# First batch's q and k loaded two rows to a partition, a second triangular selection in place of value differences, one more probability buffer, and a new order of the steps

## The chip, the cores and the metric

The kernel runs on one core of one Trainium2 chip. The time is that of one execution on the device in microseconds; the comparison is between the medians of runs of the two kernels. TensorE is called PE below, VectorE DVE, ScalarE ACT, GpSimd POOL, and SyncE, which only starts transfers here, SP.

## What is computed

Two stages, all in fp32 with 4 batches, 768 positions, 8 heads of 64:

```python
scores = (q @ k.T) / 8                     # per batch and head, 768 x 768
keep   = (column < 4) | (0 <= row - column < 128)      # 4 sinks and a window of 128
a      = softmax(where(keep, scores, -1e9));  x = a @ v  # heads side by side: 768 x 512
logits = x @ w_gate                        # 4 experts, the best 2 of each row are kept
for e in experts:                          # causal attention of x with itself, width 64
    y = softmax(causal((x @ wq[e]) @ (x @ wk[e]).T / 8)) @ (x @ wv[e])
    out += weight_of_e * (y @ wo[e])
```

## The kernel before

The work is cut into units: for each batch four "first" units (a pair of heads each, windowed attention) and two "second" units (a pair of experts each), 768 rows as six blocks of 128. Within a first unit, rows 0 and 1 go through `edge_rows`; blocks 2 and 3, and 4 and 5, go together through `both_rows`, so there are 2 x 16 = 32 such bands. The path of a band is: `quarters` (scores by PE in quarters of the array, L1399), `pick` (a copy under a mask, DVE L1729), subtraction of the row's maximum (DVE L1737), the exponential (ACT L1741), normalizing (POOL L1754 or ACT L1752), turning the probabilities by PE (`turned`, L1458), copying them from PSUM into `pt` (L1255 on ACT, L1257 on DVE), one triangular selection by position on POOL (`tri`, L1515), and the product with v (`av`, L1425), which accumulates in PSUM.

A row of block i sees the whole band from block i-1 and block i. Both blocks' scores of a band stand in one 128 columns wide tile, each column holding either the score against block i or the one against block i-1. So the product needs p times v of the right block. Before, it is made as p @ v[i-1] plus (p below or on the diagonal) @ (v[i] - v[i-1]): `differences` makes the tile `dv` with two subtractions per unit on POOL (L1646), and the selection keeps the triangle.

The finished block of a first unit is split into a high and a low part `x` (ACT L1238, then DVE L1243); the second units start from `x` of all four head pairs of a batch: `values` (L1860), then the projections (L1833), causal attention (L1386), and `store` (L1907).

For batch 0 PE turns q and k so that the 64 head dimensions stand on partitions (`turn_by_pe`, L1458 with `ident,qn` or `ident,kn`). For the other batches DVE does it (L1356), from a load that cuts q and k into 32 x 32 blocks (L1801). Batch 0 is loaded at L1797 in packets of one row of 64 numbers, 256 bytes; the first unit in two parts, blocks 0 to 2 and 3 to 5.

**What sets the order.** Each piece of work is a `plan.step` with a priority, costs per engine, the steps it follows and the buffers it takes. `emit` walks through them once at build time and writes one fixed list per engine; on the chip each engine takes its list in order. The tables `NUDGE` (added to priorities) and `ONLY` (which engine makes a step that two could make), and the three numbers `HURRY`, `STAY` and `BULK`, set that order. A step of PE has a mode: the array whole (FULL), cut by rows, by columns, or in quarters (quad). `STAY` is what a change of mode counts in PE's choice. Where `emit` expects PE to stand idle long enough in the first 130 us, it writes matmuls of zeros into the list (`fill`, L1062 and L1065); they are executed whether PE would have waited or not. The program opens with ten more (`busy`, L1918). Step names below are those of the code; in profile rows a tile's buffer number is left out.

Of the kernel before, what the change touches and what calls it, by code (L numbers as in the profile page):

```python
# [34 lines left out]
for other in ("ROWS", "FULL", "cols", "rows"):  # L35
# [10 lines left out]
    "busy_PE": 37.0, " ": 0.6, "sink_values_DVE": 6.8, " sink_values_DVE": -44.1, " sink_values_DVE 0": -181.5,  # L46
    "load_SP": 12.0, " load_SP": 0.2, " load_SP 0": -57.6, "again_SP": -83.0, " again_SP": -96.9, " again_SP 0": 135.4,
    "sink_values_ACT": 1.6, " sink_values_ACT": -56.8, "sink_values_POOL": -1.0, " sink_values_POOL": -44.4,
    " sink_values_POOL 0": -35.3, "sink_values_SP": 6.0, " sink_values_SP": 7.2, " sink_values_SP 0": -50.3,
    "load_SPACT": -2.6, " load_SPACT": -3.7, " load_SPACT 0": -3.6, "weight_ACT": -5.3, " weight_ACT": -9.3,  # L50
# [1965 lines left out]
```

## Time and profile before

| | us |
|---|---|
| median of 3 runs | 363.29 (363.12 to 363.5) |
| the profiled execution | 362.46 |
| its span, first to last instruction | 360.7 |
| PE busy | 353.2 |
| DVE, ACT, POOL busy | 293.7, 279.3, 180.2 |

The span is what the trace shows; 1.8 us lie around it. PE counts as busy while a matmul is in its pipeline, so its share says where it had something to do, not that it ran at its peak. An engine's idle time matters only where the next link of the chain to the end is late for it.

### The profile page before, as it was taken

To read this page: it belongs to the slowest core of one execution; us is meant where nothing else is said; L and a number is where in the kernel's file an instruction comes from. 1 tells how busy PE (TensorE), PEld (TensorE's weight loads), DVE (VectorE), ACT (ScalarE), POOL (GpSimd) and SP (SyncE) were. 2 spreads that over 40 slices of the span, in tenths; PEclk is the share of its full clock that TensorE was granted. 3 is DMA by queue.
4 is the path that set the end of the run, shared out by engine and by line. 5 is a ranking of instruction groups with operands and counts; after the bars stand their busy time and mean duration, and the time that the engine had idled before them with its cause. 6 is when DMAs were issued, how large, how long until landed. Compare 5 with 4: busy or idle time off the path is not lost.

```text
span 360.7 us, 12997 instructions
## 1 busy us (share of the span) xinstructions
PE 353.2 (98%) x4650; PEld 310.8 (86%) x4650; DVE 293.7 (81%) x1276; ACT 279.3 (77%) x978; POOL 180.2 (50%) x429
## 2 busy tenths in 40 slices
...
GB/s 177 165 177 183 140 161 157 196 72 49 89 131 2 178 259 181 87 70 275 217 193 134 171 259 111 34 144 315 158 47 3 197 201 44 0 229 296 94 60 116
DMA packets 136992, 52.04 MB, mean 144 GB/s; under 512 B 122016, under 2 KB 131232, under 8 KB 136928
## 3 DMA queue, kind: packets, MB, share of 16 engines
...
q14 instruction: 27, 0.22, 0.2%
HBM read 32.84 MB, written 18.09 MB: 141 GB/s over the span
## 4 chain that ended last, share of the span: by engine, by line
PE 84%; POOL 7%; DVE 3%; DMA 2%; ACT 2%; issue 2%; SPq 0%; POOLq 0%; DVEq 0%; ACTq 0%
PE b L1425 19%; PE b L1833 19%; PE b L1907 9%; PE b L1386 9%; PE b L1860 9%; PE b L1458 7%; PE b L1399 5%; PE b L1381 3%; DMA qn<-in_q_dram 1%; PE b L1918 1%; POOL p L1693 1%; PE b L1429 1%; ACT p L1741 1%; DMA o<-in_moe_wq_dram 1%; POOL wvl L1194 1%
## 5 line engine op out<-in xcount | busy, mean ns | idle before, releaser
L1611 ACT ACTIVATE p<-p,st 128x128 f32<-128x128 f32 (+5 forms) x96 | 63.5, 664 | 8.2 <-DVE st L1603 8.2
L1741 ACT ACTIVATE p<-p,st 128x132 f32<-128x132 f32 x128 | 50.8, 401 | 7.3 <-DVE st L1737 7.1
L1603 DVE CUSTOM_DVE_ANT_0 p<-b,cmask 128x384 f32<-128x384 f32 (+3 forms) x96 | 45.5, 501 | 0.6 <-PE b L1386 0.2
L1386 PE MATMUL b<-ks,qs 64*128 64x384 f32 (+3 forms) x384 | 43.0, 339 | 0.0
L1441 POOL TENSOR_TENSOR st<-st 128x2 f32<-128x2 f32 (+1 forms) x49 | 9.5, 196 | 60.1 <-ACT p L1611 45.5
L1425 PE MATMUL b<-pt,vn 128*64 128x128 f32 x448 | 38.9, 279 | 0.1
L1255 ACT ACTIVATE pt<-b 128x256 f32<-128x256 f32 (+2 forms) x87 | 33.8, 416 | 4.4 <-PE b L1458 4.1
L1860 PE MATMUL b<-wvh,x 128*128 128x260 f32 x192 | 36.1, 286 | 0.8 <-DVE x L1243 0.8
L1458 PE MATMUL b<-ident,p 64*128 64x64 f32 x760 | 36.6, 226 | 0.0
L1257 DVE COPY pt<-b 128x256 f32<-128x256 f32 (+2 forms) x77 | 33.3, 451 | 2.7 <-PE b L1458 2.5
L1458 PEld LDWEIGHTS b<-ident,p 64*128 64x128 f32 x760 | 30.6, 138 | 5.3 <-issue 1.9
L1386 PEld LDWEIGHTS b<-ks,qs 64*128 64x128 f32 x384 | 32.0, 186 | 2.2 <-issue 0.5
L1833 PE MATMUL b<-x,wkh 128*128 128x256 f32 (+1 forms) x128 | 32.7, 342 | 0.0
L1833 PE MATMUL b<-x,wqh 128*128 128x256 f32 (+1 forms) x128 | 32.6, 340 | 0.0
L1548 DVE STREAM_TRANSPOSE u<-u 128x640 f32<-128x640 f32 (+2 forms) x36 | 28.6, 822 | 4.6 <-POOL u L1266 3.4
L1907 PE MATMUL b<-woh,y 128*128 128x512 f32 x96 | 31.5, 399 | 0.0
L1737 DVE CUSTOM_DVE_ANT_0 p<-b,pair_mask 128x132 f32<-128x132 f32 x128 | 31.4, 282 | 0.0
L1860 PEld LDWEIGHTS b<-wvh,x 128*128 128x128 f32 x192 | 30.0, 188 | 1.7 <-DVE x L1243 1.2
L1680 ACT ACTIVATE p<-p,st 128x128 f32<-128x128 f32 (+1 forms) x64 | 28.8, 452 | 2.8 <-DVE st L1675 2.6
L1515 POOL TENSOR_SCALAR_AFFINE_SELECT pt<-pt 128x512 f32<-128x512 f32 x32 | 20.2, 634 | 18.2 <-ACT pt L1255 12.0
L1754 POOL TENSOR_TENSOR p<-p,st 128x528 f32<-128x528 f32 x22 | 23.3, 1066 | 11.1 <-DVE st L1446 7.9
L1425 PEld LDWEIGHTS b<-pt,vn 128*64 128x64 f32 x448 | 25.4, 136 | 3.3 <-issue 1.4
(133 smaller groups left out, 1012.3 us busy)
## 6 DMA issues: line engine op xcount, KB each, us to landing
...
```

The costliest lines, as they stand in the source:

```text
L1255: nc.scalar.activation(dst(), src(), AF.Copy)
L1257: nc.vector.tensor_copy(dst(), src())
L1386: nc.tensor.matmul(o, self.qs.t[hs, a, qs], keys(hs, b), start=n == 0, stop=n == 2)
L1425: nc.tensor.matmul(o[e * 64:e * 64 + 64], lhs, rhs, start=e not in self.begun, stop=last and self.done == len(self.steps))
L1458: nc.tensor.transpose(t[g].t[:, n, :], x[gs], ident[gs, gs])
L1603: nc.vector.tensor_tensor_reduce(out=one(e)[:, cs], in0=s2[e].t[:, :(c1 - c0) * 128], in1=mask(c0, c1), scale=times, scalar=st.t[:, 3, es] ...
L1611: nc.scalar.activation(x, x, AF.Exp, bias=st.t[:, 0, es], scale=-1.0, accum_out=st.t[:, 1, es])
L1737: nc.vector.tensor_tensor_reduce(out=p.t[:, n, :], in0=s2[e].t[:, 248 * r:248 * r + SW], in1=pair_mask, scale=-scale, scalar=BIG, op0=OP.a ...
L1741: nc.scalar.activation(p.t[:, n, :], p.t[:, n, :], AF.Exp, bias=st.t[:, 0, n:n + 1], scale=-1.0, accum_out=st.t[:, 1, n:n + 1])
L1833: nc.tensor.matmul(t.t, w[a][:, c, es], X[b, c].t[:, x, cs], start=c == 0 and m == 0, stop=c == NCH - 1 and m == 2)
L1860: nc.tensor.matmul(t.t[:, :VW], X[b, c].t[:, a, qs], W["wv"][w][:, c, :], start=c == 0 and n == 0, stop=c == NCH - 1 and n == 2)
L1907: nc.tensor.matmul(t.t, Y[b, c].t[:, a, qs], W["wo"][w][:, c, :], start=c == 0 and n == 0, stop=c == EP - 1 and n == 2)
```

## The change

Three edits in the code, and both tables and the three numbers anew (NUDGE and ONLY are some 1,500 lines of the diff, of which the rows further down show the effect).

```diff
-HURRY = 135.22
-STAY = 76.23
-BULK = -53.3
+HURRY = 51.67
+STAY = 39.17
+BULK = -12.46
...
-             ... "p": (8, 768, F32), ...
-             "dv": (2, 512, F32), "there": (4, 1536, F32), ...
+             ... "p": (9, 768, F32), ...
+             "there": (4, 1536, F32), ...
...
             def tr():
-                for j in range(hi - lo):
-                    turned(t, j, src()[:, j, :])
+                for c in range(n):
+                    for g in range(2):
+                        for e in range(2):
+                            gs, es = slice(64 * g, 64 * g + 64), slice(64 * e, 64 * e + 64)
+                            nc.tensor.matmul(t[g].t[es, c, :], nat.t[gs, lo // 2 + c // 2, e, c % 2, :], ident[gs, gs], start=True, stop=True)
...
-            tt = plan.step(prio, {PE: 62 * (hi - lo)}, tr, ..., mode="ROWS")
+            tt = plan.step(prio, {PE: 110 * n}, tr, ..., mode="quad")
...
+        def rest():
+            nc.gpsimd.affine_select(out=pt.t[:, :4, :], in_=pt.t[:, :4, :], pattern=[[0, 4], [-1, 128]], compare_op=OP.is_ge, fill=0.0,
+                                    base=-1, channel_multiplier=1)
         below_own = plan.step(prio, {POOL: 602}, tri, moved, (), [pt])
+        above = plan.step(prio, {POOL: 602}, rest, [below_own], (), [pt])
...
-                        acc.add(i + r, e, diff[0](i + r, e) if c else value[0](i + r - 1, e), pt.t[:, 4 * c + 2 * r + e, :], r == 1 and c == 1)
+                        acc.add(i + r, e, value[0](i + r - 1 + c, e), pt.t[:, 4 * c + 2 * r + e, :], r == 1 and c == 1)
...
-            def differences():
-                for e in range(2):
-                    x = value[2][0].t
-                    nc.gpsimd.tensor_sub(dv.t[...], x[:, d0 - v0:end - v0, e, :], x[:, d0 - 1 - v0:end - 1 - v0, e, :])
...
-            for n, (a, z) in enumerate([(0, 3), (3, NB)] if whole and which < 2 else [(0, NB)]):
+            for n, (a, z) in enumerate([(0, 2), (2, NB)] if whole and which < 2 else [(0, NB)]):
...
+                        if which < 2 and by_pe:
+                            start(t.t[:, a // 2:z // 2, e].rearrange("p m j d -> p m (j d)"),
+                                  x.rearrange("(m p j) d -> p m (j d)", p=128, j=2)[:, a // 2:z // 2, :])
...
-        for a, z in cut("0 3 6" if whole else TURNS):
+        for a, z in cut("0 2 6" if by_pe else TURNS):
```

Batch 0's q and k now lie two neighbouring rows to a partition, in packets of 512 bytes, and each block is turned by four matmuls with the identity, one per quarter of the array, in place of two transposes; the copy out of PSUM puts every second column in place. The product of a band takes v of both blocks directly, with the triangle in one half of `pt` and, after a second selection on POOL, the strict rest in the other.

Counted over the two orders, PE's list has 192 matmuls for turning q and k in place of 96 transposes, 46 in place of 84 filling rows of 64 x 128 and 11 in place of 13 of 128 x 128; POOL has 32 selections more and 32 subtractions less. Changes of PE's mode (filling rows left out) are 133 before and 153 now: 23 and 33 ahead of the first row of `values`, 30 and 36 ahead of its second stretch, the one that needs the last `x` of batch 0. Ahead of that second stretch stand 150 transposes of probabilities (L1458 with `ident,p`) before and 140 now; their total is the same.

PE, from the program's start to the first scores (`b_...` are PSUM banks, L1458 and L1332 the turning of q and k). Before:

```order
L1918 MATMUL b_125<-nought 128x128 x10
L1062 MATMUL b_125<-nought 128x128 x3
L1458 MATMUL b_126<-ident,qn_65 128x64
L1458 MATMUL b_127<-ident,qn_65 128x64
L1458 MATMUL b_126<-ident,qn_65 128x64
L1458 MATMUL b_127<-ident,qn_65 128x64
L1458 MATMUL b_126<-ident,qn_65 128x64
L1458 MATMUL b_127<-ident,qn_65 128x64
L1065 MATMUL b_125<-nought 64x128 x6
```

Now:

```order
L1916 MATMUL b_124<-nought 128x128 x10
L1049 MATMUL b_124<-nought 128x128
L1332 MATMUL b_125<-ident,qn_65 64x64 x2
L1332 MATMUL b_126<-ident,qn_65 64x64 x2
L1332 MATMUL b_125<-ident,qn_65 64x64 x2
L1332 MATMUL b_126<-ident,qn_65 64x64 x2
L1052 MATMUL b_124<-nought 64x128 x4
```

Two opening rows are gone, q is turned for two blocks rather than three, and the filling behind it is shorter.

DVE, where the last low parts `x` of batch 0's fourth head pair (`x_78`) stand; `qn_65` there is q of a unit of batch 1. Before:

```order
L1443 TENSOR_REDUCE st_121<-st_121 128x4
L1356 STREAM_TRANSPOSE qn_65<-qn_65 128x384
L1243 SCALAR_TENSOR_TENSOR x_78<-b_130,x_78 128x256
L1243 SCALAR_TENSOR_TENSOR x_78<-b_128,x_78 128x256
L1737 ISA p_89,st_119<-b_126,pair_mask 128x132
```

Now:

```order
L1728 ISA p_93,st_122<-b_126,pair_mask 128x132
L1728 ISA st_122 128x1
L1230 SCALAR_TENSOR_TENSOR x_78<-b_125,x_78 128x256
L1230 SCALAR_TENSOR_TENSOR x_78<-b_130,x_78 128x256
L1440 RECIPROCAL st_122<-st_122 128x4
L1350 STREAM_TRANSPOSE qn_65<-qn_65 128x384
```

The transpose of q stood ahead of the two `x_78`, and now stands behind them.

POOL, at the first selections of the program. Before:

```order
L1228 TENSOR_TENSOR v_0_83<-v_0_83,vp 16x1024
L1646 TENSOR_TENSOR dv_98<-vn_72 128x4x64 x2
L1515 AFFINE_SELECT pt_105<-pt_105 128x512
L1515 AFFINE_SELECT pt_103<-pt_103 128x512
L1441 TENSOR_TENSOR st_124<-st_124 128x4
```

Now:

```order
L1509 AFFINE_SELECT pt_103<-pt_103 128x512
L1435 TENSOR_TENSOR st_121<-st_121 128x4
L1513 AFFINE_SELECT pt_103<-pt_103 128x512
L1684 TENSOR_SCALAR p_89<-p_89,st_121 128x128 x2
L1317 COPY kx_81<-kx_81 128x5x4
```

The two subtractions of `dv` are gone, and each `pt` is selected from twice, one after the other.

## Rows read from the trace of the kernel before

**Rows 1.** The page: busy time of each engine, its share of the span, and its instructions.

```profile
PE 353.2 (98%) x4650; PEld 310.8 (86%) x4650; DVE 293.7 (81%) x1276; ACT 279.3 (77%) x978; POOL 180.2 (50%) x429
```

**Rows 2.** Busy time in six stretches of the span: stretch, its length, then busy us (and instructions) of PE, PE's weight loads, DVE, ACT and POOL, PE's granted clock, mean busy share of the DMA engines, GB/s.

```profile
0.00:7.00 7.00, 5.88 (x32) 5.77 (x32) 3.73 (x26) 1.28 (x1) 3.81 (x20) 1.00 0.87 166
7.00:20.00 13.00, 12.59 (x258) 10.57 (x256) 9.68 (x53) 9.29 (x40) 3.86 (x9) 1.00 0.93 174
20.00:40.00 20.00, 19.06 (x352) 16.12 (x348) 18.06 (x101) 19.41 (x83) 16.43 (x31) 1.00 0.81 172
40.00:63.00 23.00, 22.03 (x378) 19.16 (x378) 20.21 (x102) 21.82 (x93) 22.54 (x45) 1.00 0.82 154
63.00:351.00 288.00, 287.68 (x3619) 254.69 (x3618) 241.58 (x999) 224.71 (x757) 133.59 (x326) 1.00 0.56 141
351.00:360.70 9.70, 5.92 (x26) 4.44 (x24) 0.42 (x1) 2.77 (x5) 0.00 (x0) 1.00 0.28 108
```

**Rows 3.** The chain that ended last, in order of time, around the second stretch of `values`: start, us, what.

```profile
55.05 0.70 POOL wql L1194
...
56.07 2.98 DMA o<-in_moe_wq_dram
59.07 2.65 DMA qn<-in_q_dram
61.84 0.58 DVE qn L1356
62.79 5.66 PE b L1860 x45
68.45 8.44 PE b L1833 x48
```

**Rows 4.** DVE's instructions in order of time at that place: start, us, line, operation, out<-in, shapes, count; in brackets the idle time before, and what ended it.

```profile
61.84 0.58 DVE L1356 STREAM_TRANSPOSE qn<-qn 128x384 f32<-128x384 f32 x1 [1.53 <-DMA qn<-in_q_dram]
62.35 0.72 DVE L1243 SCALAR_TENSOR_TENSOR x<-b,x 128x256 fp32r<-128x256 f32 x2
```

**Rows 5.** PE's first instruction of the second stretch of `values`, in the same view.

```profile
62.79 0.39 PE L1860 MATMUL b<-wvh,x 128*128 128x260 f32 x1 [0.82 <-DVE x L1243]
```

**Rows 6.** Groups of PE's instructions by line and shape: count, busy us, mean ns, idle time before. A filling row of the order is two instructions here.

```profile
L1065 PE MATMUL b<-nought 128*64 128x128 f32 x168 | 11.3, 278 | 0.0
L1399 PE MATMUL b<-kx,qn 64*64 64x196 f32 x256 | 26.0, 334 | 0.1
L1458 PE MATMUL b<-ident,qn 64*128 64x64 f32 x48 | 3.1, 231 | 0.1
L1458 PE MATMUL b<-ident,kn 64*128 64x64 f32 x48 | 2.7, 231 | 0.0
```

**Rows 7.** PE's instructions in order of time, at the opening and where q and k are turned: start, us, line, operation, count.

```profile
1.11 4.64 PE L1918 MATMUL b<-nought 128*128 128x128 f32 x20 [1.11 <-DVE lanes L1118]
5.55 1.28 PE L1062 MATMUL b<-nought 128*128 128x128 f32 x6
6.75 0.40 PE L1458 MATMUL b<-ident,qn 64*128 64x64 f32 x6
7.08 0.88 PE L1065 MATMUL b<-nought 128*64 128x128 f32 x12
7.89 0.40 PE L1458 MATMUL b<-ident,kn 64*128 64x64 f32 x6
...
19.70 3.01 PE L1065 MATMUL b<-nought 128*64 128x128 f32 x52
22.64 0.59 PE L1458 MATMUL b<-ident,kn 64*128 64x64 f32 x12
23.06 0.74 PE L1458 MATMUL b<-ident,qn 64*128 64x64 f32 x12
...
26.25 1.58 PE L1399 MATMUL b<-kx,qn 64*64 64x196 f32 x48
27.76 2.19 PE L1065 MATMUL b<-nought 128*64 128x128 f32 x36
```

**Rows 8.** The same view where PE changes its mode: products by columns, transposes by rows, scores in quarters.

```profile
53.72 0.39 PE L1425 MATMUL b<-pt,vn 128*64 128x128 f32 x4
53.94 0.39 PE L1425 MATMUL b<-pt,dv 128*64 128x128 f32 x4
54.26 0.27 PE L1458 MATMUL b<-ident,psk 64*128 64x64 f32 x2
54.37 0.41 PE L1458 MATMUL b<-ident,p 64*128 64x64 f32 x8
54.62 0.87 PE L1381 MATMUL b<-kx,qn 64*128 64x128 f32 x8
...
55.39 0.42 PE L1458 MATMUL b<-ident,p 64*128 64x64 f32 x8
55.73 1.71 PE L1399 MATMUL b<-kx,qn 64*64 64x196 f32 x48
```

**Rows 9.** Groups of POOL's instructions over the span: count, busy us, mean ns, idle time before them and what ended it.

```profile
L1646 POOL TENSOR_TENSOR dv<-vn 128x256 f32<-128x256 f32 x32 | 22.8, 730 | 0.9 <-DMA vn<-in_v_dram 0.4 <-PE b L1425 0.2 <-DMA kn<-in_k_dram 0.2
L1515 POOL TENSOR_SCALAR_AFFINE_SELECT pt<-pt 128x512 f32<-128x512 f32 x32 | 20.2, 634 | 18.2 <-ACT pt L1255 12.0 <-DVE pt L1257 5.0 <-DMA kn<-in_k_dram 0.6
```

**Rows 10.** The same two groups from 20 to 62.8 us.

```profile
L1515 POOL TENSOR_SCALAR_AFFINE_SELECT pt<-pt 128x512 f32<-128x512 f32 x8 | 5.0, 631 | 0.0
L1646 POOL TENSOR_TENSOR dv<-vn 128x256 f32<-128x256 f32 x6 | 4.2, 724 | 0.1
```

**Rows 11.** POOL in order of time around its first subtractions.

```profile
8.71 0.20 POOL L1329 COPY kx<-kx 128x20 f32<-128x20 f32 x1 [3.71 <-ACT kx L1255]
8.87 1.41 POOL L1646 TENSOR_TENSOR dv<-vn 128x256 f32<-128x256 f32 x2
14.64 0.72 POOL L1693 TENSOR_SCALAR p<-p,st 128x128 f32<-128x128 f32 x2 [4.36 <-ACT qn L1255]
```

**Rows 12.** Transfers of the first 8 us that the tile `qn` takes part in: the six issues on SP's queue (issuing time in ns, min, median, max; first and last start), and the time from issue to landing.

```profile
L1797 SPq DMA_DIRECT2D qn<-in_q_dram x6: 445/488/922, 0.8 to 5.4; - x6
...
DMA to landing us min/median/max: 2.6/3.0/3.4
```

More of the change, by code (lines that the diff above doesn't have):

```diff
@@ L45 @@
 NUDGE = {
[L46 to L50, printed above, removed]
@@ new lines @@
+    "000 fn_DVEACT 16": ACT, "000 fn_DVEACT 17": ACT, "010 load_SPACT 0": SP, "010 load_SPACT 1": SP,
+    "010 load_SPACT 2": SP, "010 fn_DVEACT 1": ACT, "010 fn_DVEACT 6": DVE, "010 total_DVEPOOL 0": POOL,
+    "010 norm_POOLACT 0": POOL, "010 norm_POOLACT 1": ACT, "010 fn_DVEACT 8": DVE, "010 fn_DVEACT 9": DVE,
+    "010 total_DVEPOOL 1": DVE, "010 norm_POOLACT 2": POOL, "010 fn_DVEACT 12": ACT, "010 norm_POOLACT 3": POOL,
+    "010 fn_DVEACT 14": ACT, "010 fn_DVEACT 16": DVE, "010 fn_DVEACT 17": ACT, "020 load_SPACT 0": SP,
@@ new lines @@
+    "020 load_SPACT 2": SP, "020 fn_DVEACT 0": DVE, "020 fn_DVEACT 1": ACT, "020 fn_DVEACT 3": ACT, "020 fn_DVEACT 4": ACT,
+    "020 fn_DVEACT 5": DVE, "020 norm_POOLACT 1": POOL, "020 fn_DVEACT 8": DVE, "020 total_DVEPOOL 1": POOL,
+    "020 fn_DVEACT 10": DVE, "020 fn_DVEACT 11": ACT, "020 fn_DVEACT 12": DVE, "020 fn_DVEACT 13": DVE,
+    "020 total_DVEPOOL 2": DVE, "020 norm_POOLACT 3": ACT, "020 fn_DVEACT 16": DVE, "030 load_SPACT 1": SP,
+    "030 load_SPACT 2": SP, "030 fn_DVEACT 4": DVE, "030 fn_DVEACT 5": DVE, "030 norm_POOLACT 0": ACT,
@@ new lines @@
+    "030 fn_DVEACT 8": ACT, "030 fn_DVEACT 9": DVE, "030 fn_DVEACT 11": ACT, "030 fn_DVEACT 12": DVE,
+    "030 norm_POOLACT 3": POOL, "030 fn_DVEACT 14": ACT, "030 fn_DVEACT 16": ACT, "030 fn_DVEACT 17": ACT,
+    "110 load_SPACT 0": SP, "110 load_SPACT 1": SP, "110 total_DVEPOOL 0": DVE, "110 total_DVEPOOL 1": DVE,
+    "110 norm_POOLACT 2": ACT, "110 fn_DVEACT 4": ACT, "110 total_DVEPOOL 2": POOL, "110 norm_POOLACT 3": POOL,
+    "110 fn_DVEACT 7": DVE, "100 load_SPACT 0": SP, "100 load_SPACT 1": SP, "100 load_SPACT 2": SP,
@@ new lines @@
+    "100 norm_POOLACT 0": ACT, "100 norm_POOLACT 1": ACT, "100 fn_DVEACT 1": ACT, "100 total_DVEPOOL 1": POOL,
+    "100 norm_POOLACT 2": ACT, "100 fn_DVEACT 2": DVE, "100 fn_DVEACT 4": DVE, "100 fn_DVEACT 5": DVE,
+    "100 total_DVEPOOL 2": DVE, "100 fn_DVEACT 7": DVE, "100 fn_DVEACT 9": ACT, "001 fn_DVEACT 1": ACT,
+    "001 fn_DVEACT 3": DVE, "001 fn_DVEACT 4": DVE, "001 total_DVEPOOL 0": POOL, "001 norm_POOLACT 0": ACT,
+    "001 fn_DVEACT 6": ACT, "001 fn_DVEACT 7": ACT, "001 total_DVEPOOL 1": POOL, "001 fn_DVEACT 8": ACT,
@@ new lines @@
+    "120 fn_DVEACT 5": ACT, "120 total_DVEPOOL 2": POOL, "120 fn_DVEACT 7": ACT, "120 fn_DVEACT 8": ACT,
+    "130 load_SPACT 0": SP, "130 load_SPACT 1": SP, "130 load_SPACT 2": SP, "130 norm_POOLACT 0": POOL,
+    "130 norm_POOLACT 1": POOL, "130 fn_DVEACT 0": ACT, "130 fn_DVEACT 1": DVE, "130 total_DVEPOOL 1": POOL,
+    "130 norm_POOLACT 2": POOL, "130 fn_DVEACT 4": DVE, "130 norm_POOLACT 3": POOL, "130 fn_DVEACT 7": ACT,
+    "130 fn_DVEACT 8": DVE, "011 norm_POOLACT 0": POOL, "011 norm_POOLACT 1": ACT, "011 norm_POOLACT 2": ACT,
@@ new lines @@
+    "011 total_DVEPOOL 2": POOL, "011 norm_POOLACT 5": POOL, "011 fn_DVEACT 1": ACT, "011 total_DVEPOOL 3": POOL,
+    "011 norm_POOLACT 6": ACT, "011 fn_DVEACT 3": ACT, "011 total_DVEPOOL 5": DVE, "011 norm_POOLACT 10": ACT,
+    "011 fn_DVEACT 4": DVE, "011 fn_DVEACT 6": DVE, "011 store_SPACT 0": SP, "011 fn_DVEACT 7": ACT,
+    "011 store_SPACT 2": SP, "011 store_SPACT 3": ACT, "011 store_SPACT 4": SP, "011 store_SPACT 5": SP,
+    "210 load_SPACT 1": SP, "210 load_SPACT 2": SP, "210 norm_POOLACT 1": POOL, "210 fn_DVEACT 0": DVE,
@@ new lines @@
+    "210 norm_POOLACT 2": ACT, "210 fn_DVEACT 5": DVE, "210 norm_POOLACT 3": POOL, "210 fn_DVEACT 9": ACT,
+    "200 load_SPACT 1": SP, "200 load_SPACT 2": SP, "200 norm_POOLACT 0": POOL, "200 norm_POOLACT 1": ACT,
+    "200 fn_DVEACT 0": ACT, "200 fn_DVEACT 1": ACT, "200 total_DVEPOOL 1": DVE, "200 fn_DVEACT 2": ACT,
+    "200 fn_DVEACT 3": ACT, "200 fn_DVEACT 5": ACT, "200 norm_POOLACT 3": POOL, "200 fn_DVEACT 6": DVE,
+    "200 fn_DVEACT 7": ACT, "200 fn_DVEACT 9": ACT, "101 fn_DVEACT 1": DVE, "101 fn_DVEACT 2": ACT, "101 fn_DVEACT 4": DVE,
@@ new lines @@
+    "220 load_SPACT 2": SP, "220 fn_DVEACT 0": DVE, "220 fn_DVEACT 1": ACT, "220 norm_POOLACT 2": POOL,
+    "220 fn_DVEACT 3": ACT, "220 fn_DVEACT 5": DVE, "220 norm_POOLACT 3": POOL, "220 fn_DVEACT 7": ACT,
+    "220 fn_DVEACT 9": DVE, "230 load_SPACT 0": ACT, "230 load_SPACT 2": SP, "230 norm_POOLACT 1": ACT,
+    "230 fn_DVEACT 0": ACT, "230 fn_DVEACT 1": ACT, "230 norm_POOLACT 2": POOL, "230 fn_DVEACT 2": ACT,
+    "230 fn_DVEACT 3": ACT, "230 total_DVEPOOL 2": POOL, "230 fn_DVEACT 6": DVE, "230 fn_DVEACT 9": DVE,
@@ new lines @@
+    "111 norm_POOLACT 1": ACT, "111 total_DVEPOOL 1": POOL, "111 norm_POOLACT 2": ACT, "111 norm_POOLACT 3": POOL,
+    "111 norm_POOLACT 4": ACT, "111 fn_DVEACT 0": ACT, "111 total_DVEPOOL 3": DVE, "111 norm_POOLACT 7": POOL,
+    "111 norm_POOLACT 9": ACT, "111 fn_DVEACT 3": ACT, "111 norm_POOLACT 11": ACT, "111 fn_DVEACT 4": ACT,
+    "111 fn_DVEACT 5": DVE, "111 store_SPACT 0": ACT, "111 fn_DVEACT 7": DVE, "111 fn_DVEACT 8": ACT,
+    "111 fn_DVEACT 9": ACT, "111 store_SPACT 3": SP, "111 store_SPACT 4": SP, "111 fn_DVEACT 11": ACT,
@@ new lines @@
+    "300 load_SPACT 0": SP, "300 load_SPACT 1": SP, "300 total_DVEPOOL 0": POOL, "300 norm_POOLACT 1": POOL,
+    "300 fn_DVEACT 0": ACT, "300 fn_DVEACT 1": DVE, "300 total_DVEPOOL 1": DVE, "300 fn_DVEACT 2": DVE,
+    "300 fn_DVEACT 3": ACT, "300 fn_DVEACT 4": ACT, "300 fn_DVEACT 5": ACT, "300 total_DVEPOOL 2": DVE,
+    "300 norm_POOLACT 3": POOL, "300 fn_DVEACT 6": ACT, "201 fn_DVEACT 0": ACT, "201 fn_DVEACT 1": ACT,
+    "201 fn_DVEACT 2": ACT, "201 fn_DVEACT 4": DVE, "201 fn_DVEACT 5": ACT, "201 norm_POOLACT 0": ACT,
@@ new lines @@
+    "310 norm_POOLACT 1": POOL, "310 fn_DVEACT 0": DVE, "310 total_DVEPOOL 1": DVE, "310 norm_POOLACT 2": ACT,
+    "310 fn_DVEACT 5": ACT, "310 norm_POOLACT 3": POOL, "320 load_SPACT 0": SP, "320 load_SPACT 1": SP,
+    "320 load_SPACT 2": SP, "320 norm_POOLACT 2": POOL, "320 fn_DVEACT 4": ACT, "320 total_DVEPOOL 2": POOL,
+    "320 norm_POOLACT 3": ACT, "320 fn_DVEACT 6": ACT, "320 fn_DVEACT 7": ACT, "320 fn_DVEACT 8": ACT,
+    "320 fn_DVEACT 9": DVE, "330 total_DVEPOOL 0": POOL, "330 norm_POOLACT 0": ACT, "330 norm_POOLACT 1": POOL,
@@ new lines @@
+    "330 fn_DVEACT 0": ACT, "330 total_DVEPOOL 1": DVE, "330 norm_POOLACT 2": POOL, "330 fn_DVEACT 2": DVE,
+    "330 fn_DVEACT 5": ACT, "330 fn_DVEACT 7": DVE, "330 fn_DVEACT 8": ACT, "330 fn_DVEACT 9": ACT,
+    "211 norm_POOLACT 0": ACT, "211 norm_POOLACT 1": POOL, "211 total_DVEPOOL 2": POOL, "211 norm_POOLACT 4": ACT,
+    "211 fn_DVEACT 0": ACT, "211 fn_DVEACT 1": ACT, "211 norm_POOLACT 6": ACT, "211 norm_POOLACT 8": POOL,
+    "211 norm_POOLACT 9": POOL, "211 fn_DVEACT 2": DVE, "211 fn_DVEACT 3": ACT, "211 total_DVEPOOL 5": DVE,
@@ new lines @@
+    "211 norm_POOLACT 10": POOL, "211 norm_POOLACT 11": POOL, "211 fn_DVEACT 4": ACT, "211 fn_DVEACT 6": ACT,
+    "211 store_SPACT 0": ACT, "211 fn_DVEACT 7": DVE, "211 store_SPACT 1": SP, "211 fn_DVEACT 8": DVE,
+    "211 store_SPACT 2": SP, "211 fn_DVEACT 9": DVE, "211 store_SPACT 3": ACT, "211 fn_DVEACT 10": DVE,
+    "211 store_SPACT 4": SP, "211 fn_DVEACT 11": DVE, "301 fn_DVEACT 3": ACT, "301 fn_DVEACT 4": ACT,
+    "301 fn_DVEACT 5": ACT, "301 norm_POOLACT 0": POOL, "301 norm_POOLACT 1": POOL, "301 total_DVEPOOL 1": POOL,
@@ new lines @@
+    "301 total_DVEPOOL 2": DVE, "301 norm_POOLACT 4": POOL, "301 fn_DVEACT 7": ACT, "301 norm_POOLACT 7": POOL,
+    "301 fn_DVEACT 8": ACT, "301 fn_DVEACT 9": ACT, "301 total_DVEPOOL 5": POOL, "301 fn_DVEACT 10": ACT,
+    "311 total_DVEPOOL 0": POOL, "311 norm_POOLACT 1": ACT, "311 fn_DVEACT 0": DVE, "311 fn_DVEACT 1": ACT,
+    "311 total_DVEPOOL 1": POOL, "311 norm_POOLACT 2": ACT, "311 fn_DVEACT 2": ACT, "311 fn_DVEACT 3": DVE,
+    "311 norm_POOLACT 4": ACT, "311 norm_POOLACT 5": POOL, "311 fn_DVEACT 4": ACT, "311 fn_DVEACT 5": DVE,
```

187 lines of the change are left out of this document (60 added, 127 removed), and 1335 rows, old and new, of the table NUDGE.

## Prediction, made before the changed kernel was run

> **What bounds the kernel now.** I read the busy shares first: PE is busy 98% of the span, DVE 81%, ACT 77%, POOL 50% [rows 1]. A share is an average, so the table by stretches comes next [rows 2], and it shows three stages. From 63 to 351 us PE is busy for 287.68 of 288 us: there only PE's own instructions count. From 20 to 63 us ACT is busy for 19.41 of 20 and 21.82 of 23 us, POOL for 22.54 of the last 23, DVE for some nine tenths. PE looks just as full there, but part of its list is matmuls of zeros: 168 instructions, 84 rows, 11.3 us [rows 6]. So in the early stage PE is not the bound; the softmax of batch 0 on ACT, DVE and POOL is. From 351 us on comes a tail in which PE ends. The granted clock is 1.00 in all six stretches.
>
> The chain that ended last shows the seam of the first two stages [rows 3]: a transfer of q, its transpose on DVE at 61.84, then PE's second stretch of `values` at 62.79, and behind it PE without a break. In order of time, DVE stood still 1.53 us for that transfer with the two `x` queued behind the transpose [rows 4], and PE stood 0.82 us for those `x` [rows 5]. The working splits at this point: when does the last `x` of batch 0 come, and how much PE work lies after it?
>
> **PE's instructions.** Filling: 38 rows of 64 x 128 fewer, 11.3 / 84 = 0.135 us each [rows 6]: **−5.1**. Opening: 2 rows of 128 x 128 fewer; three took 6.75 − 5.55 = 1.20 us [rows 7], 0.40 each: **−0.8**. No wait stands between them and the turning of q at 6.75, so they set its start. The first four issues begin 0.5 us apart from 0.8 on, and landing takes up to 3.4 us [rows 12]; the part of q needed first should be there by 1.3 + 3.4 = 4.7, ahead of 5.95.
>
> Turning q and k: 96 transposes go. Twelve took 23.06 − 22.64 = 0.42 us, 35 ns each [rows 7], so 96 took 3.4 us. In their place come 384 quarter matmuls of 64 columns (192 rows of the order, x2). The trace has no such turning. Per quarter they move 48 blocks x 64 columns x 2 instructions = 6144 columns. Below: the four quarters run side by side at the pace of the filling, 128 columns in 0.135 / 2 = 0.067 us, 0.52 ns a column: 3.2 us. Above: nothing runs side by side and each instruction takes the 31 to 35 ns of a transposing one, 384 x 31.5 = 12.1 us. The nearest row is the band scores, the same quarters and type: 48 instructions from 26.25 to 27.76, 1.51 us [rows 7], which is 4 rows of 196 columns x 2 = 1568 columns per quarter, 0.96 ns a column. 6144 x 0.96 = 5.9 us, so **+2.5** (−0.2 to +8.7).
>
> Here the Trainium skill speaks against the change: "TensorE: Matmul & The Clock Gate", the part on packing small matmuls by row and column tiling, its mechanism, says that a weight load overlaps matmuls in flight only when its row group differs. Two quarters of one row group would then take turns, load and product one behind the other; that is the third rival below. The trace does not look like it: at 0.52 ns a column one band score of 196 columns takes 0.10 us, so 48 of them two at a time would need 2.4 us, and they took 1.51 [rows 7].
>
> Mode changes: four products took 0.22 us without one behind them (53.72 to 53.94) and 0.32 with one (53.94 to 54.26); eight transposes 0.25 without (54.37 to 54.62) and 0.34 with (55.39 to 55.73) [rows 8]. So 0.10 each, and 20 more: **+2.0**, of which 6 ahead of the second stretch of `values` and 14 behind.
>
> Products: 64 with `dv` become 64 with `vn`, same shape, nothing. PE's list: −5.1 − 0.8 + 2.5 + 2.0 = **−1.4**; with the 0.8 of standing [rows 5] −2.2.
>
> **When the last x comes.** By PE's list alone it would be 62.8 − 5.9 (filling and opening) + 2.5 + 0.6 (six changes) − 0.8 (standing) − 0.35 (ten transposes of p at 35 ns moved behind) = 58.9. But filling covers waits, and the bound there is ACT and DVE. Weighing the instructions ahead of the last `x` in each list with the mean duration of their groups gives ACT 49.7 before and 51.1 us now, DVE 51.9 and 52.9: work was drawn forward, +1.4 on the fuller engine. Against it stand 0.8 from the opening, 0.8 from the `x` that no longer queue behind the transpose, and ACT's idle time between 7 and 63 us, 3.7 + 0.6 + 1.2 = 5.5 us [rows 2]. Most of it lies before 20 us, where ACT waits for q and k, and there the first unit now starts with two blocks. How much goes no row shows: between none and all I take about half, 2.6. So 62.8 − 0.8 − 0.8 + 1.4 − 2.6 = **60.0**, 2.8 earlier; of the filling saved, 1.1 us returns as bare waiting of PE.
>
> **After it**, PE-bound: 14 changes x 0.10 = +1.4 and ten transposes +0.35. Sum: −2.8 + 1.75 = **−1.05**. The profiled execution took 362.46, of which 360.7 are span; it becomes 361.4. The median of the runs is 0.83 above the profiled one, so the median becomes **362.2**.
>
> **At no cost.** POOL: 32 subtractions, 22.8 us, out and 32 selections like those of 20.2 us in, −2.6 [rows 9]; after 63 us POOL has 154 us idle [rows 2], so neither gain nor the wait of a product for its second selection (0.63) shows, except in 40 to 63 (second rival). If that cover failed, each of the 24 bands after batch 0's eight would cost up to 0.63, 15 us; the 18.2 us idle ahead of selections [rows 9] says that POOL waits for them, not PE for it. The ninth `p` lets a subtraction start earlier; it helps only where DVE waits for a buffer, at most DVE's 2.8 idle in 40 to 63 [rows 2], which I count in the half above. The loads by pairs all on SP's queue: k's first parts are the third and fourth issue, 0.8 + 3 x 0.5 + 3.4 = 5.7 us, ahead of the turning of k at some 7.1 (7.89 less 0.8) [rows 7, 12]; if late, the 0.8 of the opening is lost. The tail keeps its steps.
>
> **Rivals.**
> 1. *The early stage gives the filling back.* ACT's idle time shrinks by 1.4 only, as much as its list has grown; `x` comes at 62.8 − 1.6 = 61.2, −1.6 + 1.75 = +0.15: **363.4**. For it: ACT and POOL full in 20 to 63. Against: 3.7 us idle in 7 to 20.
> 2. *Slower: POOL's two selections in series.* Each product of a band now waits for two of them, 1.27 us, where `dv` could be made ahead; the first `dv`, at 8.87, lay in idle time [rows 11] and saved nothing by going. In 20 to 62.8 six subtractions (4.2) go and eight selections (5.0) come [rows 10], +0.8, and the last product waits 0.63 longer: `x` 1.4 later than in rival 1, 62.6: −0.2 + 1.75 = +1.55, **364.8**. It decides once `x` is later than 62.8 − 1.75 + 0.7 = 61.8. For it: POOL 22.54 of 23. Against: it had 3.6 us idle in 20 to 40 [rows 2].
> 3. *Quarters take turns.* Per block two row groups of four matmuls, one behind the other with their loads, 70 ns each (two transposing instructions): 280 ns x 48 = 13.4, less 3.4 is +10 in place of 2.5: **369.7**. The band scores speak against it, as above.
> 4. *PE's list alone counts.* The waits do not come back, `x` at 58.9: −3.9 + 1.75 = −2.2, **361.1**; with the cheapest turning 358.4.
> 5. *The clock falls* to 1.2 GHz where filling is gone. No row has a stretch below 1.00, so its price is open: each us of PE's work there takes two, five of them give above 367.
>
> **Chances.** Forecast .33 (its own range 361.4 to 362.9), rival 1 .28, 2 .18, 3 .03, 4 .15, 5 .03. About 0.2%, 0.73 us, is what a measurement of this kernel can tell from no change. Faster than 362.56: .27 of the forecast, rival 4, .04 of rival 1, .46. Within: .06 + .20 + .02, .28. Slower: .04 + .16 + .06, .26. The range reaches from rival 4 with turning 0.9 cheaper, 360.2, to rival 2 with 0.4 more, 365.2.
>
> **What would show it.** The second stretch of `values` at about 60.0, with DVE not standing ahead of `x`; turning at 0.12 us a block (eight instructions) where blocks stand together; PE waits of about 1 us between 7 and 60; 63 to 351 full as now; POOL's selections 0.63 each, PE waiting for `pt` by POOL nowhere after 63. Wrong if `x` comes after 61.8, if a block's turning takes over 0.2 us, if PE stands for the second selection, or if 288 us of PE-bound work holds more than the 14 changes.

## The result and the profile after

The changed kernel takes 367.6 us (median of 4 runs, 366.73 to 370.18), the kernel before in the same comparison 363.21: 4.4 us more, ratio 1.0132 (95% interval 1.0101 to 1.0164). The forecast was 362.2 with a range to 365.2, so both the direction and the range were wrong. The profiled execution has a span of 365.0 us where the one before had 360.7. The longest of the four runs, 370.18, had a mean granted clock of 0.99; the other three, 366.73 to 368.23, had 0.998 to 1.00. By the interval of the ratio the change costs 3.7 to 6.0 us, and some of that can be the clock.

The busy shares of the page:

```profile
PE 354.5 (97%) x4858; PEld 310.0 (85%) x4858; DVE 288.4 (79%) x1255; ACT 277.9 (76%) x991; POOL 181.8 (50%) x437
```

The six stretches, with the columns of [rows 2]; the last ends with the span:

```profile
0.00:7.00 7.00, 5.89 (x42) 5.55 (x44) 3.73 (x26) 1.41 (x2) 3.81 (x20) 1.00 0.54 148
7.00:20.00 13.00, 12.50 (x372) 10.73 (x370) 9.65 (x54) 9.34 (x40) 3.99 (x10) 1.00 0.89 223
20.00:40.00 20.00, 18.55 (x472) 15.47 (x472) 19.54 (x103) 19.49 (x88) 16.40 (x35) 1.00 0.71 147
40.00:63.00 23.00, 21.71 (x347) 19.23 (x339) 20.99 (x104) 23.00 (x99) 20.30 (x40) 1.00 0.89 173
63.00:351.00 288.00, 285.57 (x3538) 250.79 (x3538) 232.03 (x967) 220.59 (x760) 137.25 (x335) 1.00 0.54 138
351.00:365.00 14.00, 10.31 (x108) 8.21 (x104) 2.51 (x5) 4.08 (x8) 0.00 (x0) 1.00 0.30 114
```

Against [rows 1] PE has hardly more to do. Against [rows 2] the early stage is bound as forecast: ACT is busy for 23.00 of 23 us from 40 to 63, POOL less than before. The new thing is in the long stretch, where by the prediction "only PE's own instructions count": 285.57 busy of 288 where 287.68 were, and at its end more work is left (10.31 us of PE behind 351, before 5.92). PE waits there now. What PE waited for over the span, in us, times, longest (changed kernel):

```profile
PE b L1419 <- DMA u<-there: 2.0, 2, 1.6
PE b L1423 <- DVE sk L1244: 1.2, 1, 1.2
...
PE b L1419 <- POOL pt L1513: 0.9, 2, 0.6
PE b L1393 <- DVE kx L1244: 0.6, 2, 0.4
PE b L1423 <- POOL vs L1636: 0.5, 1, 0.5
```

`u` are probabilities of the second units that are transposed by way of memory: SP writes them to `there` and loads them back, and a product of PE uses them. This is a wait that the prediction did not name; before it was 0.2 us. The second selection (L1513) accounts for 0.9 us only, of which 0.3 behind 63 us. The waits of L1423 and L1393 lie ahead of 63 us.

When did the second stretch of `values` come? PE in order of time, before and then changed:

```profile
61.34 0.39 PE L1860 MATMUL b<-wvh,x 128*128 128x260 f32 x1
61.56 0.29 PE L1860 MATMUL b<-wvl,x 128*128 128x260 f32 x1
61.69 0.28 PE L1860 MATMUL b<-wvh,x 128*128 128x260 f32 x1
```

```profile
60.99 0.39 PE L1858 MATMUL b<-wvh,x 128*128 128x260 f32 x1
61.22 0.29 PE L1858 MATMUL b<-wvl,x 128*128 128x260 f32 x1
61.34 0.40 PE L1858 MATMUL b<-wvh,x 128*128 128x260 f32 x2
```

Three instructions of the stretch could be made ahead of the late `x`; the fourth waited to 62.79 before [rows 5] and follows without a wait at 61.46 now (the second of the x2 in the last line). From this fourth instruction, which I call "the x" below, I split all runs: the x 1.33 us earlier than in the profile before, then 299.46 us to the start of PE's last instruction (360.92) where before had 293.74 (62.79 to 356.53). So −1.3 early, +5.7 late, +4.4 in all. This compares one execution with one: with the list of before the x came at 61.8 and 61.7 in two later executions (e7, e8 below), with the changed list at 60.45 and 61.08 (e6, e12).

### The profile page after: what moved, and what is told of

It reads as the page before. It is cut to its first block, busy times and chain, and to the rows that moved or that the text cites. A ratio compares the mean times of both kernels' runs of the same rounds, so it can differ in the third digit from the quotient of the medians.

```text
span 365.0 us, 13404 instructions
## 1 busy us (share of the span) xinstructions
PE 354.5 (97%) x4858; PEld 310.0 (85%) x4858; DVE 288.4 (79%) x1255; ACT 277.9 (76%) x991; POOL 181.8 (50%) x437
## 4 chain that ended last, share of the span: by engine, by line
PE 72%; ACT 10%; DMA 5%; DVE 4%; POOL 3%; issue 1%; SPq 1%; POOLq 0%; DVEq 0%; ACTq 0%
PE b L1419 15%; PE b L1831 15%; PE b L1858 10%; PE b L1905 9%; PE b L1380 8%; PE b L1452 6%; ACT p L1732 4%; PE b L1393 4%; DMA u<-there 2%; PE b L1375 2%; ACT p L1671 2%; DMA qn<-in_q_dram 2%; PE b L1423 1%; PE b L1332 1%; DMA there<-u 1%
## 5 line engine op out<-in xcount | busy, mean ns | idle before, releaser
L1610 ACT ACTIVATE p<-p,st 128x384 f32<-128x384 f32 (+5 forms) x96 | 63.7, 668 | 7.0 <-DVE st L1602 4.5
L1419 PE MATMUL b<-pt,vn 128*64 128x128 f32 x704 | 46.7, 278 | 1.0 <-POOL pt L1513 0.9
L1419 PEld LDWEIGHTS b<-pt,vn 128*64 128x64 f32 x704 | 37.8, 137 | 5.2 <-POOL pt L1513 1.6
L1380 PE MATMUL b<-ks,qs 64*128 64x384 f32 (+3 forms) x384 | 41.9, 339 | 0.0
L1242 ACT ACTIVATE pt<-b 128x256 f32<-128x256 f32 (+3 forms) x103 | 38.4, 408 | 2.4 <-PE b L1452 2.3
L1858 PE MATMUL b<-wvh,x 128*128 128x260 f32 x192 | 36.9, 285 | 0.0
L1905 PE MATMUL b<-woh,y 128*128 128x512 f32 x96 | 32.4, 400 | 0.0
L1244 DVE COPY pt<-b 128x256 f32<-128x256 f32 (+3 forms) x61 | 27.7, 467 | 0.6 <-PE b L1452 0.4
```

The source lines that it names most:

```text
L1242: nc.scalar.activation(dst(), src(), AF.Copy)
L1380: nc.tensor.matmul(o, self.qs.t[hs, a, qs], keys(hs, b), start=n == 0, stop=n == 2)
L1419: nc.tensor.matmul(o[e * 64:e * 64 + 64], lhs, rhs, start=e not in self.begun, stop=last and self.done == len(self.steps))
L1610: nc.scalar.activation(x, x, AF.Exp, bias=st.t[:, 0, es], scale=-1.0, accum_out=st.t[:, 1, es])
L1858: nc.tensor.matmul(t.t[:, :VW], X[b, c].t[:, a, qs], W["wv"][w][:, c, :], start=c == 0 and n == 0, stop=c == NCH - 1 and n == 2)
L1905: nc.tensor.matmul(t.t, Y[b, c].t[:, a, qs], W["wo"][w][:, c, :], start=c == 0 and n == 0, stop=c == EP - 1 and n == 2)
```

## The experiments

To change one thing and nothing else, the order that `emit` makes was written out and put in place of the planner: the same instructions on each engine in the same order and the same buffers, but for the edit.

```diff
     def emit(self):
-        ... (the walk over priorities and costs)
+        for name, eng, slots in ORDER:      # step, engine, buffers, as emit had made them
+            s = by.pop(name); s.eng = eng
+            for b, (tag, n) in zip(s.new, slots): b.slot = n
+            order.append(s)
```

All were compared with the kernel before on the same chip; its median was 362.53 to 362.64 in these comparisons, and "above" is the distance to it. The changed kernel is 4.4 above in its own comparison. Each of these figures is good to about 1 us (last column). A difference of under 2 us between two runs, against the changed kernel above all, is shown only where the traces show it too.

| run | order | edit | median | above | ratio (95%) |
|---|---|---|---|---|---|
| e1 | before | second selection | 367.0 | 4.5 | 1.0128 (1.0103 to 1.0153) |
| e2 | before | pairs of rows | 365.05 | 2.5 | 1.0067 (1.0046 to 1.0088) |
| e3 | before | both | 369.93 | 7.4 | 1.0202 (1.0177 to 1.0228) |
| e4 | new | pairs of rows undone | 365.15 | 2.6 | 1.0096 (1.0062 to 1.013) |
| e5 | new | second selections left out | 368.75 | 6.1 | 1.0168 (1.0148 to 1.0188) |
| e6 | new | a load of q on SP later | 365.85 | 3.2 | 1.0099 (1.0073 to 1.0124) |
| e7 | before | 64 filling rows, mode kept | 368.63 | 6.0 | 1.0167 (1.0146 to 1.0188) |
| e8 | before | 64 filling rows, 64 changes of mode | 377.71 | 15.1 | 1.0416 (1.0395 to 1.0436) |
| e9 | before | q's transpose behind the last x | 364.01 | 1.4 | 1.0037 (1.0022 to 1.0052) |
| e10 | before | no filling | 365.05 | 2.5 | 1.0059 (1.0025 to 1.0092) |
| e11 | before | e1, triangle's products first | 364.97 | 2.4 | 1.0066 (1.0052 to 1.008) |
| e12 | new | a load of q on ACT later | 364.68 | 2.05 | 1.0063 (1.0048 to 1.0078) |
| e13 | new | e12, e4 and e11 together | 362.73 | 0.1 | 0.9999 (0.9983 to 1.0015) |

### Which part costs: e1 to e4

> The kernel before, with every engine's list held in the order of before, and one edit alone: the second selection in place of the differences (each second selection stands right behind its first, the 32 subtractions are left out). Theory O, the loss of 4.4 us comes from the new order: 362.9 to 364.0, since products wait for the second selection only where POOL is full, before the last x of batch 0. Theory C, the loss comes from the edits in the code: 365 to 367, with PE waiting for pt by POOL in many places after 63 us.

> The kernel before in the order of before, with the other edit alone: batch 0's q and k loaded as pairs of rows, turned in quarters, first parts of two blocks; filling as before. Theory O: 362.5 to 365.5, since turning measured some 6 us in the changed kernel against 3.4 before and the filling that stood for this time is still in the list, so up to 2.5 come on top before the last x, and nothing behind it changes. Theory C: 365.5 to 367, and the stretch behind the last x is longer too.

> All of the changed kernel's code (both edits) in the order of before. It differs from the changed kernel by the order alone. Theory O: 362.5 to 365.5, from the last x of batch 0 to PE's last instruction as long as before (294 us; the changed kernel needs 299.5). Theory C: 366.5 to 368, as the changed kernel.

> The changed kernel in its own new order, with the pairs of rows undone: loads of one row a partition, parts of three and three blocks, transposes as before. Theory O: 366 to 368, the 5.5 us lost behind the last x stay. Theory C: 363 to 365.

Theory O, which has in common with the prediction that a product waits for its second selection only where POOL is full, fell on e1 and e3. (e2 came out within its range, e3 above the range of either theory, and e4 0.15 above that of theory C.) The second selection alone costs 4.5 us, the pairs of rows alone 2.5, both 7.4. **The new order does not lose, it wins 3.0 of it back** (7.4 to 4.4). In the traces it wins 5.2 ahead of the x (66.65 in e3, 61.46 now) and loses 2.0 behind it (297.43 and 299.46). Undoing the pairs in it gives back 1.8 (4.4 to 2.6); the intervals of the two runs overlap, but in the traces the x comes 1.75 earlier and the stretch behind it is the same to 0.3 us. e2's trace has the x at 62.98, 0.2 later than the profile before, and 1.9 us more behind it, 1.0 of it in waits; theory O expected nothing there. e1's trace splits as the x at 64.11 (+1.3) and 297.02 us behind it (+3.3). There PE's list and order are those of before, so the two traces can be laid side by side instruction by instruction: behind the x, five products start 0.22, 0.51, 0.46, 0.50 and 0.60 us later against the one ahead of them, 2.3 us, each a product that waits for a selection; the other 1.0 is the net of pieces of 0.1 to 0.25, longer and shorter. What PE waited for in e1:

```profile
PE b L1425 <- POOL pt L1519: 4.0, 7, 1.3
```

One of the five places, POOL and then PE in e1 (L1519 is the second selection):

```profile
197.66 0.64 POOL L1515 TENSOR_SCALAR_AFFINE_SELECT pt<-pt 128x512 f32<-128x512 f32 x1
198.37 0.64 POOL L1519 TENSOR_SCALAR_AFFINE_SELECT pt<-pt 128x512 f32<-128x512 f32 x1
...
199.06 1.20 PE L1425 MATMUL b<-pt,vn 128*64 128x128 f32 x18 [0.44 <-POOL pt L1519]
```

And the same place before:

```profile
195.09 0.39 ACT L1255 ACTIVATE pt<-b 128x256 f32<-128x256 f32 x1
...
195.28 0.20 POOL L1441 TENSOR_TENSOR st<-st 128x2 f32<-128x2 f32 x1 [1.94 <-ACT p L1611]
195.55 0.64 POOL L1515 TENSOR_SCALAR_AFFINE_SELECT pt<-pt 128x512 f32<-128x512 f32 x1
...
196.44 0.44 PE L1425 MATMUL b<-pt,vn 128*64 128x128 f32 x4
```

This is the reading that the prediction missed. POOL stands idle 1.94 us shortly ahead of the selection, and yet the selection has no slack: ACT's copy into `pt` ends at 195.48, the selection begins at 195.55, ends at 196.19, and PE's product starts at 196.44. Another 0.64 us behind it ends at 199.01 in e1, and the product starts at 199.06. **POOL's idle time says that POOL is fed late, not that its result is early.**

### Latency, or load of POOL: e11

```diff
-            for r in range(2):
-                for c in range(2):
+            for c in (1, 0):
+                for r in range(2):
                     for e in range(2):
                         acc.add(i + r, e, value[0](i + r - 1 + c, e), pt.t[:, 4 * c + 2 * r + e, :], ...)
```

> The first experiment again (order of before, second selection alone, 367.0), with the product of a band in another order inside: first the four pairs that need the triangle (ready after the first selection), then the four that need the rest (after the second). If the 4.5 us are the latency of two selections in a row ahead of the product: 364 to 365.8, since 0.44 us of products now lie beside the second selection. If they come from POOL's load or from the differences no longer made: 366.5 to 367.5.

2.4 above in place of 4.5. POOL's list is the same as in e1; only the product's first half no longer needs the second selection. In the trace PE waits 0.6 us for a selection, once, where e1 had 4.0 in seven. So the waits, and about half of e1's cost, are the latency of two selections in a row ahead of a product. The other 2.4 us are not explained by them: e11's x comes at 62.99, 0.2 later than before, and the stretch behind it is 3.0 us longer, of which PE's waits for `u` (1.0 where 0.2 were) show only a part; the rest lies in small pieces, and no run tells their cause.

### The second selection in the new order: e5

```diff
         def rest():
-            nc.gpsimd.affine_select(out=pt.t[:, :4, :], in_=pt.t[:, :4, :], ...)
+            pass
```

> The changed kernel in its own order, with the 32 second selections left out of the program (the half of pt that they would mask stays unmasked). Theory S, the second selection is what costs, in the new order too, since the order had to be bent round it but its latency stays: 364 to 365.5, at least 2 us less than the changed kernel. Theory M, the new order hides the second selection (only 0.9 us of waits for it are in the changed kernel's trace) and pays for that with mode changes and waits elsewhere: 366.3 to 367.6, at most 1.3 us less.

No gain; the median is 1.7 worse, in overlapping intervals. Beside the changed kernel's trace, the wait for a second selection at 275.02 (0.38) is gone, and one for `u` at 226.05 (0.46), but three waits for `u` stand there, 3.8 us in all:

```profile
PE b L1419 <- DMA u<-there: 3.8, 3, 2.2
```

So the new order does hide the second selection behind the x, as theory M has it (the time itself came out above the range of either theory), and PE, when it comes sooner, only meets the next late thing, `u`. Why `u` came later in this run, also around 305 us (1.31 and 0.64 us more than in the changed kernel), no run tells; it stays open.

### What a change of mode costs: e7 and e8

```diff
+                ["FILL", "cols", bank, 1]    # two rows of 64 x 128, at 32 places between 64 and 335 us
```

In e7 the places are between two steps by columns, in e8 between two steps by rows; the work added is the same.

> The kernel before in its own order, with 64 more filling rows of 64 x 128 between 64 and 335 us, two at each of 32 places where PE works by columns ahead and behind, so no change of mode is added. At 0.135 us a row 8.6 us more: 371 to 372.5, a little less where a wait is covered.

> The same 64 filling rows, two at each of 32 places where PE works by rows ahead and behind, so each place adds two changes of mode, 64 in all. At 0.10 us a change (the prediction's price) 6.4 us above the run with the rows in place without changes: 377.5 to 379. At 0.15 us 9.6 above it. If changes cost nothing by themselves: the same time as that run.

64 rows cost 6.0 us, 0.094 each, less than expected (in the traces 7.3 behind the x, 0.11 each, and the x came 1.0 earlier than in the profile before). The 64 changes cost 15.1 − 6.0 = 9.1 us, **0.14 us each**, where the prediction took 0.10; behind the x the two traces differ by 9.2. e8's median lies in the range of 0.10 only because e7 came out below its own. The 64 are changes between rows and columns. The new order has 14 more changes behind the x, 6 of this kind, the others from or to the whole array or quarters, whose price was not measured; at 0.14 all of them are 2.0 us, an estimate.

### What the early stage gives: e9 and e10

```diff
-L1356 STREAM_TRANSPOSE qn_65<-qn_65 128x384
 L1243 SCALAR_TENSOR_TENSOR x_78<-b_130,x_78 128x256
 L1243 SCALAR_TENSOR_TENSOR x_78<-b_128,x_78 128x256
+L1356 STREAM_TRANSPOSE qn_65<-qn_65 128x384
```

> The kernel before in its own order, with one DVE instruction moved: the transpose of q behind the last two x of batch 0, and not ahead of them. If the 1.5 us that DVE stood for that transfer, and the 0.8 us of PE behind it, belong to every execution: 361.3 to 362.0, 0.8 less than before. If they were a late transfer in the one profiled execution (two later kernels with the same list up to there had the x at 61.7 and 61.8): 362.3 to 362.9, no change.

Slower by 1.4, which neither theory had. First, the wait at the x is not in every execution: e7 and e8 have the list of before up to there, and in both the x came at 61.8 and 61.7, with no wait of PE. In e9 the transfer of q was late again, landing by 62.14, so it can be late under both lists. DVE at this place in e7, where the transfer of q was in time (compare [rows 4], where it ended 1.53 us of waiting):

```profile
60.45 0.58 DVE L1356 STREAM_TRANSPOSE qn<-qn 128x384 f32<-128x384 f32 x1
60.96 0.71 DVE L1243 SCALAR_TENSOR_TENSOR x<-b,x 128x256 fp32r<-128x256 f32 x2
```

Second, what is gained at the x is taken back: in e9 the x comes at 61.98, 0.8 earlier than in the profile before, and 16 us later PE waits for `qs`, which DVE makes. The stretch behind the x is 2.4 us longer than before; this wait and 0.5 more for `u` account for 1.5 of it, the rest stays open.

```profile
PE b L1386 <- DVE qs L1317: 1.0, 2, 0.9
```

> The kernel before in its own order, with all filling behind the opening left out (84 rows of 64 x 128 and 3 of 128 x 128). The prediction's account: filling stands in waits, and of each us saved a part returns as waiting; all 12.5 us gone could bring x to 59 to 61 at best, 360 to 362. If ACT and DVE set the x: 362.3 to 363. If the granted clock falls where the filling is gone: above 363.5, with a clock below 1.00 in 7 to 40 us.

The third case. All of the filling gone, the stretches of e10 from 20 us on:

```profile
20.00:40.00 20.00, 16.89 (x217) 13.41 (x219) 15.95 (x90) 17.77 (x75) 15.21 (x29) 0.74 0.74 146
40.00:63.00 23.00, 22.85 (x404) 19.73 (x402) 21.20 (x104) 22.01 (x94) 22.06 (x45) 1.00 0.80 155
```

The granted clock is 0.74 on the mean of 20 to 40 us, so part of this stretch ran at 1.2 GHz, and the x came at 63.67. With the 46 rows that the changed kernel keeps it is 1.00 in its profile. The runs of e10 lie far apart, and go by the clock: four with a mean of 0.995 over the span took 361.96 to 362.42, 0.2 to 0.6 less than the kernel before; eight with 0.965 to 0.986 took 364.13 to 367.38. The 23 runs of the kernel before beside them had 0.998 or more. So without the filling the time is at best a little shorter, and where the clock falls it is up to 5 us longer.

### What holds u back: e6 and e12

The chain that ended last in the changed kernel, in order of time at PE's longest wait:

```profile
139.32 3.21 DMA qn<-in_q_dram
142.53 0.02 issue
142.54 0.30 SPq L1554
142.84 0.04 issue
142.89 2.65 DMA u<-there
145.54 0.24 issue
145.78 1.09 PE b L1419 x16
```

SP's eight issues of `u`, and what SP waited for between 130 and 146 us:

```profile
134.12 9.20 SPq L1554 DMA_DIRECT2D u<-there  x8
...
SPq L1554 <- DMA qn<-in_q_dram: 3.5, 1, 3.5
```

SP held the last two of eight loads of `u` until 142.54, the moment a transfer of q landed. First I took SP's own queue for the cause.

```diff
 SP:
-    300 load q     (ahead of the three groups of u<-there)
     011 back 1, 011 back 2
+    300 load q
```

> The changed kernel in its own order, with one load of q (unit 300, four transfers) issued behind, and not ahead of, the three groups of loads of transposed probabilities that PE waited 1.6 us for at 145.8 us; its two transposes on DVE a little later. If SP's queue held those loads back: 365.5 to 366.3, and the wait at 145.8 gone. If the round trip through memory itself is late: 367 to 368 and the wait stays.

The wait did not go: 2.2 us at 145.36. The time fell in the range of the theory that its trace refutes, by luck: it is 1.2 us better than the changed kernel's, and in this profile the x comes 1.0 earlier with the same list up to there, while the stretch behind it is as long (299.69). The transfer in question was another, on ACT's queue.

```diff
 ACT:
-    230 load q     (four transfers at 139.3)
     ...
+    230 load q
```

> The changed kernel in its own order, with the load of q for unit 230 (four transfers on ACT's queue at 139.3 us) and its two transposes moved 13 us and more back. In three kernels of the new order SP issued the last two loads of transposed probabilities within 0.02 us of the landing of that load's first transfer, and PE waited for them 1.5 to 2.4 us. If that load holds them back: the wait at 145.8 goes, 365.3 to 366.4. If the two only meet by chance: 367 to 368, the wait stays.

2.05 above in place of 4.4, better than expected. In the traces the stretch behind the x is 1.7 us shorter (297.79), which is the wait; the x, 0.4 earlier, is not the edit's. PE in e12 and SP's issues of `u`; in the changed kernel PE waited at this place until 145.78:

```profile
143.43 0.85 PE L1419 MATMUL b<-pt,v 128*64 128x128 f32 x12
144.08 1.07 PE L1419 MATMUL b<-u,v 128*64 128x128 f32 x16
...
133.64 5.29 SPq L1554 DMA_DIRECT2D u<-there  x8
```

So a load on one queue delays issues on the other. The records of the traces show the link: each transfer signals its landing by a semaphore (a counter that an engine can wait for), and the transfers of SP and ACT share eight of them. The issue that SP held until 142.54 waits for semaphore 104, its own, which q's transfer that landed at 142.53 signals; e4, e5 and e6 show the same pair at this place (in e6 with 109). In e12 SP waits for no transfer of q between 130 and 146 us, and PE's wait is gone.

### Do the terms add up: e13

> The new order with what the experiments gave: that load of q later, transposes of one row a partition in place of the quarters, and the triangle's products ahead of the rest's. If the terms add up: 367.6 less 2.45 (old turning) less 1.5 (load) less 0.4 (order inside the product), 363.2, between 362.5 and 364. If one early gain is only a wait at the next place: 364 to 365.5.

4.4 − 1.8 (e4) − 2.35 (e12) leave 0.25 above, less what e11 gives in this order; measured 0.1. With terms that are good to about 1 us, so close a sum is partly luck. In the trace PE is busy again for 287.82 of 288 us from 63 to 351. It also shows what the new order costs PE when nothing waits: the x comes at 59.73, and from there PE needs 297.20 us with 0.2 of waiting, before 293.74 with 0.3. That is 3.5 us more. No run here is measurably faster than the kernel before. Putting the differences back into the new order was not tried.

## Why the prediction was wrong, point by point

**The second selection at no cost: the step that failed most.** The sentence "POOL waits for them, not PE for it" drew slack from idle time. Measured alone: 4.5 us (e1). Rival 2 had the mechanism (two selections in series), the price early (x +1.4; e1's profile shows +1.3), but only "in 40 to 63"; 3.3 of e1's 4.5 came behind 63 us, where POOL was thought to be cover enough, and its total, 364.8, was 2.8 short. e11 shows about half of the 4.5 to be the two selections in a row ahead of a product; the other half is open. The bound given for a failed cover, 15 us, was far above.

**"After it", PE-bound, +1.75: the other step that failed.** Measured +5.7 behind the x, in two parts. PE's own work there is some 3.5 more (e13, where nothing waits), twice the forecast, and the waits are the rest. As far as it can be split (waits from start to start): 14 changes of mode at 0.14, 2.0 (mis-sized: 1.4); ten transposes, 0.35; waits for `u`, 1.8 and 0.46, and one for the second selection, 0.38, less 0.3 that was there before, 2.3 (not in the sum). About 1 us stays; the scores of the causal attention (`ks`, `qs`), 31.5 us from start to start before and 32.8 now, are 1.2 of the difference (part of it can be changes of mode), and why they are slower no run tells. PE's 287.68 of 288 busy does not say that nothing else would be late if PE came sooner: `qs` (e9, 77.9 us) and `u` (144 to 146 us) were just in time. In e4 the x came at 59.71, 1.75 earlier than in the changed kernel, and PE then stood 1.3 us for this group of `u`; in e5 and e6 it stood 2.2. What is gained early is partly lost there, until the load that holds `u` back is moved (e12).

**The x at 60.0.** Measured 61.46, and 60.45 and 61.08 in two more executions with the same list up to there. Of the 2.8 us forecast, 0.8 was a transfer that is late in some executions only (e7, e8); against the x of those without it, 61.7 to 61.8, the three executions of the changed list gain 0.2 to 1.4. ACT's list and the turning ate the rest: ACT's idle time from 7 to 63 us is 3.66 + 0.51 + 0.00 = 4.2 us now, 1.3 less than before, where 2.6 less was taken. That is rival 1's early stage (61.2, idle time less by 1.4), which was right for this stage and had the total wrong for the reason above.

**Turning +2.5: right as a price, wrong as covered.** The changed kernel's PE, four blocks of q:

```profile
9.18 0.69 PE L1332 MATMUL b<-ident,qn 64*64 64x64 f32 x32
9.69 0.65 PE L1332 MATMUL b<-ident,kn 64*64 64x64 f32 x32
```

32 instructions in 0.51 us, 0.13 a block (forecast 0.12), so rival 3, load and product of a row group (quarters on the same rows of the array) one behind the other at 0.28, is out; the Trainium skill's rule on weight loads ("TensorE: Matmul & The Clock Gate", the part on packing small matmuls), read as the prediction read it, does not describe this turning. Whether all four quarters compute at once is not shown: the products alone, two at a time at the filling's 0.52 ns a column, would also need 8 x 64 x 0.52 / 2 = 0.13 us a block, an estimate. Nor could the band scores show it, as the prediction had it: it took all 48 instructions for 196 columns wide, and two thirds are narrower.

```profile
L1399 PE MATMUL b<-kx,qn 64*64 64x196 f32 x256 | 26.0, 334 | 0.1
L1399 PE MATMUL b<-kx,qn 64*64 64x128 f32 x256 | 22.5, 269 | 0.0
L1399 PE MATMUL b<-kx,qn 64*64 64x68 f32 x256 | 19.3, 227 | 0.0
```

With equal thirds of 196, 128 and 68 columns, two at a time would need 1.6 us for the 48, not 2.4, against the 1.51 measured. In time the turning cost 2.5 (e2) and 1.8 (new order), not the part of it that the filling should have covered.

**The chances.** The filling account (−5.1) was next to no gain: with all of it gone and the clock nearly kept, e10 is 0.2 to 0.6 below the kernel before, and in eight runs of twelve the clock falls. That is rival 5, which had three in a hundred. In the changed kernel's profile it did not happen, but one of its four runs had 0.99 and took 370.18, and e4, with the same 46 rows, took 367.4 and 367.9 in the two of six runs with 0.994 and 0.995, 364.6 to 365.2 in the others. So rival 5 may hold a part of the 4.4; how much, four runs do not tell. Rival 4, PE's list alone, is refuted by the waits. The order, which I costed only as mode changes and a moved transpose, is what hid most of the second selection (from e3 to the changed kernel PE's waits for it fall from 4.1 us to 0.9, and the time by 3.0), and its price is those changes and the late `u`.
